# Tile 0 normalized in two parts and tile 1 in one, the bias row loaded behind W2's second half, and a new written order

## The chip, the cores and the metric

The kernel runs on one core of one Trainium2 chip. Its engines are TensorE (PE, with its weight loads shown apart as PEld), VectorE (DVE), ScalarE (ACT), GpSimd (POOL) and SyncE (SP), which issues nearly all DMAs. The metric is the device time of one execution in microseconds (us); lower is better.

## The reference

```python
def _A_ref(x, w_r, w_i):                  # x: 2048 x 640
    X = rfft2(x.astype(float32), axes=(-2, -1))
    X = X * (w_r + 1j * w_i)              # 2048 x 321
    return irfft2(X, s=(S, D), axes=(-2, -1)).astype(bfloat16)

def _B_ref(x, w1, b1, w2, b2):
    h = gelu_tanh(einsum("bsd,df->bsf", x, w1) + b1)    # 640 -> 1536
    return einsum("bsf,fd->bsd", h, w2) + b2            # 1536 -> 640

xn = layernorm(x)                         # over the 640 columns
return x + _A_ref(xn, A_w_r, A_w_i) + _B_ref(xn, B_w1, B_b1, B_w2, B_b2)
```

All inputs and outputs are bf16. The output is the input plus a spectral filter of the normalized input plus a two-layer network on the normalized input.

## The kernel before

The 2048 rows are 16 tiles of 128 rows, two tiles to a pair. Each step has a name, and the names carry tile, group or block numbers:

- `x4` loads tiles of the input; `w1_00` to `w1_14` load W1 in ten chunks (half, fifth of the contraction); `w2_0` and `w2_1` load W2 in two halves; `bias2` loads b2 to all partitions; `W..` load the spectral weights.
- `st`, `ag` (DVE) are mean and variance; `sq`, `rs` the reciprocal deviation (for tiles 0 and 1 on ACT and DVE, later on POOL); `nm` (line 555, DVE) subtracts the mean and multiplies, and writes the normalized tile.
- A normalized tile is transposed: tiles 0 to 3 on PE (`tp`, line 569) into a PSUM bank, which `tc` (line 423 on ACT or 424 on DVE) copies to xnT; tiles 4 to 15 by DMA (`td`, line 561).
- `h` are the matmuls of the first layer. Blocks 0 and 1 are single tiles, and their matmuls have 128 columns: `h0.2.1` is block 0, bank 2 of four, fifth 1 of the contraction, three matmuls. Later blocks have two or four tiles. `ge` (ACT) are the gelus, `b1mm` and `b1cp` bring the bias b1 into place for them.
- `f1`, `f2` (DVE), `G` (PE), `gx`, `b`, `xb`, `c`, `y`, `m`, `z`, `d`, `u`, `vt`, `e`, `yo`, `y2`, `yf` are the spectral path, forward and back.
- `k` (ten tiles, early) and `l` (six tiles, late) are the matmuls of the second layer, `kk` (DVE) parks a `k` result with the residual added; `fin` (PE) is the last spectral step of one piece of a tile, `os` (line 810, DVE) adds it up into one of four staging slots, and `out` (SP) stores it. A tile's `os` waits until the store that used its slot before has landed.

Every step is recorded with what it reads and writes. The order of the steps on each engine is not found by a scheduler when the program is built: it is written out by hand in the table `ORDER` (engine and name, one after the other), and a second table, `SLOTS`, gives each step its PSUM bank or buffer slot. From these the program works out the semaphore waits. An engine runs its list strictly in order, so a waiting step holds all that is behind it. A `gate` bears on what order is admissible and gives no wait of its own.

Before the first real matmul, PE runs nine matmuls on zeros (`idle0`).

Of the kernel before, what the change touches and what calls it, by code (L numbers as in the profile page):

```python
# [13 lines left out]
D = 640  # L14
# [228 lines left out]
PARTS = (0, 1, 3, 5)  # L243
# [10 lines left out]
pool:xbpad2b sp:x0 dve:warm0 act:bias1 pool:xbpad0b dve:eps5 pool:xbpad1a pool:id0 pe:idle0 pool:id1 act:table0 sp:x1 pool:xbpad1b pool:xbpad2a  # L254
pool:wpad sp:w1_00 pool:mhalf pool:xbpad0a sp:w1_01 sp:w1_02 sp:x2 dve:st0.0 dve:st0.1 sp:w1_03 dve:st1.0 sp:w1_04 dve:ag0 dve:st1.1 sp:x3 act:sq0
dve:rs0 sp:w1_10 pe:b1mm dve:ag1 dve:nm0 dve:nm0.1 act:sq1 pe:tp0.0 act:b1cp dve:nm0.3 sp:w1_11 pe:tp0.1 dve:rs1 dve:tc0.0 pe:tp0.3 dve:nm1.1
act:tc0.1 sp:w1_12 pe:h0.0.0 dve:nm1 dve:nm1.3 pe:tp1.1 act:tc0.3 pe:h0.1.0 sp:w1_13 dve:f10.1 pe:tp1.0 act:tc1.1 pe:tp1.3 pe:h0.1.1 act:tc1.0
pe:h0.0.1 dve:f10.0 sp:w1_14 act:table1 pe:h0.0.2 pe:h1.0.0 dve:st2.0 sp:x4 pe:h1.0.1 pe:h1.0.2 pe:h0.1.2 dve:st2.1 sp:x6 pe:h0.1.3 pe:h0.0.3
dve:f20.00 pe:h0.1.4 sp:g act:tc1.3 pe:h1.1.0 dve:ag2 pe:h1.1.1 dve:st3.0 sp:x8 pe:h1.1.2 pe:h1.0.3 dve:ve2 pe:h1.0.4 dve:st3.1 sp:x10 pool:rs2
pe:h1.2.0 pe:h0.3.0 act:ge1.1 pe:h0.2.0 sp:x12 dve:ag3 act:ge1.0 pe:h0.2.1 dve:f20.11 dve:ve3 pe:h1.1.3 act:ge0.3 dve:nm2 pe:h1.2.1 pool:rs3 act:ge1.2  # L260
pe:h1.3.0 dve:f20.10 pe:h1.3.1 act:ge0.4 pe:h1.3.2 dve:f20.01 pe:h1.3.3 dve:nm3 pe:tp2.0 pe:h1.1.4 dve:f11.0 pe:h0.2.2 act:tc2.0 pe:h1.2.2 pe:h1.2.3
dve:f11.1 pe:h0.0.4 act:ge1.4 pe:h0.3.1 pe:tp3.0 dve:st4.0 pe:h0.3.2 dve:st5.1 pe:h0.3.3 act:tc3.0 pe:h1.2.4 pe:h1.3.4 dve:st5.0 pe:h0.3.4 act:ge0.5
pe:h0.2.3 dve:st4.1 pe:h2.0.0 act:ge0.0 act:ge0.1 dve:ag5 pe:h2.0.3 dve:ag4 act:ge0.11 pe:h0.2.4 dve:ve4 pe:h2.4.0 dve:st6.0 act:ge1.6 pool:rs4
pe:h2.4.3 act:ge1.5 dve:st6.1 pe:h2.1.0 act:ge1.3 act:ge0.10 pe:h2.1.3 dve:nm4 act:ge0.7 pe:h2.5.0 dve:st7.1 act:ge1.8 sp:td4 pe:h2.2.0 act:ge1.11
dve:nm5 pe:h2.2.3 act:ge1.7 pe:h2.3.0 dve:f21.10 act:ge0.8 pe:h2.3.3 dve:ag6 dve:st8.0 pe:h2.6.0 act:ge2.3 sp:td5 pe:h2.6.3 dve:st7.0 pe:h2.5.3
act:ge2.2 pe:h2.7.0 dve:f21.00 act:ge0.9 pe:h2.7.3 dve:f21.01 act:ge0.6 dve:f21.11 pe:h2.10.0 dve:ag7 act:ge0.2 dve:st11.1 sp:x14 pe:h2.10.3 act:ge2.7
pe:h2.11.0 dve:st10.1 sp:w2_0 act:ge2.6 pe:h2.11.3 dve:f12.0 act:ge2.4 pe:G0 sp:W10n dve:ve6 pe:h2.8.0 act:ge2.5 dve:st8.1 pool:rs6 pe:G1 act:ge2.0
dve:st12.1 pe:h2.8.3 dve:nm6 act:ge2.1 pe:h2.9.0 dve:nm7 act:ge2.10 pe:h2.9.3 dve:st10.0 pe:h3.0.0 act:gx0.0 pe:h3.6.0 pe:h3.0.3 dve:st11.0 sp:td7
pe:h3.1.0 dve:ag10 pe:h3.6.3 dve:f12.1 act:ge2.9 pe:h3.7.0 act:ge2.8 dve:ag11 dve:f22.00 pe:h3.7.3 pe:G3 dve:ve10 sp:td6 dve:st9.1 act:ge3.7 pe:h3.4.0
pool:rs10 act:ge2.11 dve:st9.0 pe:h3.4.3 pe:h3.5.0 act:ge3.6 dve:f22.10 pe:h3.5.3 dve:f22.11 pe:G2 dve:f22.01 dve:st14.0 pe:h3.1.3 act:gx1.0 pe:h3.8.0  # L270
dve:ag9 dve:nm10 pe:h3.8.3 pe:h3.10.0 dve:nm11 sp:td10 pe:h3.10.3 dve:ag8 pe:h3.11.0 act:ge3.0 dve:ve8 dve:f13.0 pool:rs8 pe:h3.11.3 act:ge3.1
dve:f13.1 pe:G5 act:ge3.4 pe:G4 sp:td11 dve:nm8 act:ge3.5 pe:h3.2.0 dve:f23.00 pe:h3.2.3 act:gx2.0 pe:h3.3.0 dve:nm9 pe:h3.9.0 dve:st12.0 sp:td8
pe:h3.9.3 dve:f23.10 pe:k1.0.0 act:ge3.9 dve:f23.11 dve:f23.01 pe:h3.3.3 dve:st13.0 act:ge3.8 pe:k1.0.3 act:ge3.3 dve:st15.0 sp:td9 pe:k2.0.0
act:ge3.11 dve:st15.1 act:ge3.2 pe:G7 dve:st14.1 pe:G6 act:ge3.10 dve:f14.1 pe:h4.6.0 sp:bias2 act:ge1.10 dve:f14.0 pe:h4.6.3 act:ge1.9 sp:w2_1
pe:h4.7.0 act:gx3.0 dve:f24.10 pe:h4.4.0 sp:W10m dve:st13.1 pe:h4.7.3 pe:h4.4.3 dve:ag12 sp:m pe:k2.0.3 dve:f24.00 act:ge4.7 dve:f24.11 sp:W12p
act:ge4.6 dve:f24.01 pe:h4.5.0 dve:ag13 dve:ag14 pe:h4.5.3 dve:f15.0 sp:W00p pe:h4.10.0 act:ge4.5 dve:f15.1 pe:h4.10.3 pe:h4.11.0 act:ge4.4 sp:W13p
dve:ve12 dve:f25.01 pool:rs12 dve:f25.00 pe:h4.11.3 pe:G8 sp:e dve:f25.10 act:ge4.11 pe:G9 dve:f25.11 sp:W11n act:ge4.10 pe:h5.0.0 dve:nm13 act:gx4.0
# [56 lines left out]
def bass_parallel_sum__spectral_gfnet__dense_activation_gelu__prompt_kernel(  # L334
# [516 lines left out]
```

## Time and profile before

| what | value |
|---|---|
| device time, median of 3 runs | 148.06 us (147.77 to 148.54) |
| profiled execution: its own time | 147.68 us |
| profiled execution: span from first to last instruction | 146.2 us |
| PE busy | 142.7 us, 98% of the span |
| DVE busy | 117.8 us, 81% |
| ACT busy | 80.8 us, 55% |
| DMA | 18.39 MB, mean 126 GB/s |

Busy time counts an instruction from its start to its end, and matmuls overlap, so a busy PE is no proof that it ran at its peak. In the rows below a timeline row gives start, duration, engine, line, operation, output and input, shape, count and, in brackets, the idle time before it and what ended it. A row of the chain of waits gives start, duration, and what the end of the program was then waiting for. A group row gives count, busy time, mean duration of one in ns, and idle time before it.

### The profile page before, as it was taken

Reading aid. Unit: us, or ns where it says so; the run is one execution under the profiler, and the core shown is the slowest. Engines: PE = TensorE matmul, PEld = TensorE weight load, DVE = VectorE, ACT = ScalarE, POOL = GpSimd, SP = SyncE. Lnnn points to the kernel's source line nnn. Section 1 sums busy time; section 2 is a strip of 40 time slices with the busy share of each in tenths; the row PEclk is TensorE's granted clock in tenths of the full one; section 3 lists DMA queues with packets and bytes.
Section 4 is the critical chain, followed back from the end, with each engine's and each line's share of the span. In section 5 each row is a group of like instructions: output and inputs, shape, how many; then the busy total and the mean of one; then the engine's idle time right before and its main releaser. Section 6 shows DMA issues by size and latency. Waiting matters only on the chain.

```text
span 146.2 us, 4123 instructions
## 1 busy us (share of the span) xinstructions
PE 142.7 (98%) x1727; PEld 96.2 (66%) x1727; DVE 117.8 (81%) x274; ACT 80.8 (55%) x154; POOL 6.8 (5%) x24
## 2 busy tenths in 40 slices
PE   7999999999999999999999999999999999999994
PEld 2589899887567867545555443446787767767773
DVE  2999999999879625639999888973179999699994
ACT  3586998998664735473884778774044622400000
POOL 2030111201200000000000000000000000000000
PEclk9999999999999999999999999999999999999999
DMA  4999679757999999300000677546600003031145
GB/s 141 278 348 399 196 197 289 146 104 223 242 132 208 182 160 189 121 0 4 0 4 2 42 140 121 69 90 134 125 14 0 4 0 112 25 131 53 66 159 179
DMA packets 29369, 18.39 MB, mean 126 GB/s; under 512 B 20264, under 2 KB 28200, under 8 KB 29224
## 3 DMA queue, kind: packets, MB, share of 16 engines
q1 hardware_dynamic: 29328, 18.14, 53.7%
q8 instruction: 13, 0.21, 0.6%
q14 instruction: 4, 0.03, 0.1%
q10 hardware_dynamic: 24, 0.00, 0.0%
HBM read 10.92 MB, written 2.62 MB: 93 GB/s over the span
## 4 chain that ended last, share of the span: by engine, by line
PE 92%; DMA 3%; SPq 3%; issue 0%; DVE 0%
PE ps L413 91%; DMA W<-in_B_w_dram 3%; SPq L408 3%; PE ps L569 0%; DVE W L810 0%
## 5 line engine op out<-in xcount | busy, mean ns | idle before, releaser
L413 PE MATMUL ps<-W,gT 128*128 128x384 bf16 (+3 forms) x396 | 59.5, 296 | 0.0
L413 PE MATMUL ps<-xnT,W 128*128 128x256 bf16 (+2 forms) x420 | 59.0, 289 | 0.1
L413 PEld LDWEIGHTS ps<-W,gT 128*128 128x128 bf16 x396 | 36.4, 98 | 17.5 <-issue 1.9
L413 PEld LDWEIGHTS ps<-xnT,W 128*128 128x128 bf16 x420 | 34.6, 98 | 14.6 <-issue 1.2
L639 ACT ACTIVATE gT<-ps,b1col 128x256 bf16<-128x256 f32 (+2 forms) x84 | 36.9, 522 | 7.0 <-PE ps L413 6.9
L523 DVE BATCH_NORM_STATS2 U<-X 128x6 f32<-128x320 bf16 x32 | 14.0, 478 | 2.2 <-DMA X<-in_A_x_dram 2.1
L800 DVE TENSOR_TENSOR xnT<-ps,X 128x384 f32<-128x384 f32 (+1 forms) x16 | 7.8, 485 | 7.1 <-PE ps L413 7.1
L423 ACT ACTIVATE T<-ps 128x644 bf16<-128x644 f32 (+2 forms) x19 | 10.5, 595 | 5.0 <-PE ps L413 4.8
L423 ACT ACTIVATE Wf<-ps 128x960 bf16<-128x960 f32 (+1 forms) x8 | 6.7, 867 | 9.8 <-PE ps L413 9.8
L423 ACT ACTIVATE XV<-ps 128x1280 bf16<-128x1280 f32 (+1 forms) x8 | 9.6, 1202 | 0.5 <-PE ps L413 0.4
L584 DVE TENSOR_TENSOR T<-T 128x512 bf16<-128x512 bf16 (+1 forms) x32 | 9.0, 315 | 0.1
L423 ACT ACTIVATE Xb<-ps 128x960 bf16<-128x960 f32 x4 | 5.1, 1265 | 6.4 <-PE ps L413 6.4
L810 DVE TENSOR_TENSOR W<-ps,xnT 128x256 bf16<-128x256 f32 (+1 forms) x16 | 7.4, 485 | 0.7 <-PE ps L413 0.5
L555 DVE TENSOR_SCALAR T<-X,mv,rstd 128x640 bf16<-128x640 bf16 (+2 forms) x20 | 7.4, 406 | 0.7 <-POOL rstd L534 0.6
L424 DVE CAST T<-ps 128x644 bf16<-128x644 f32 x5 | 4.1, 827 | 4.7 <-PE ps L413 4.7
L413 PE MATMUL ps<-Wf,htab 128*128 128x384 bf16 (+3 forms) x33 | 7.5, 295 | 0.0
L699 DVE TENSOR_TENSOR T<-T 128x644 bf16<-128x644 bf16 x16 | 7.4, 488 | 0.2
L413 PE MATMUL ps<-EB,XV 32*128 32x160 bf16 (+1 forms) x128 | 7.2, 232 | 0.0
L580 DVE TENSOR_TENSOR T<-T 128x640 bf16<-128x640 bf16 x16 | 7.1, 479 | 0.1
L534 POOL TENSOR_TENSOR rstd<-ve,mhalf 128x2 f32<-128x2 f32 (+1 forms) x8 | 5.7, 710 | 31.0 <-DVE ve L533 31.0
L768 DVE TENSOR_TENSOR Wf<-Wf 128x960 bf16<-128x960 bf16 (+1 forms) x12 | 6.9, 596 | 0.1
L413 PEld LDWEIGHTS ps<-EB,XV 32*128 32x128 bf16 (+1 forms) x128 | 5.6, 95 | 2.1 <-ACT U L423 0.4
(62 smaller groups left out, 127.3 us busy)
## 6 DMA issues: line engine op xcount, KB each, us to landing
out_dram<-W SPq DMA_DIRECT2D x15, 160.0 KB, 1.9
W<-in_B_w_dram SPq DMA_DIRECT2D x10, 192.0 KB, 4.4
X<-in_A_x_dram SPq DMA_DIRECT2D x6, 320.0 KB, 6.0
W<-in_B_w_dram SPq DMA_DIRECT2D x2, 960.0 KB, 8.4
Wf<-in_A_w_i_dram SPq DMA_DIRECT2D x7, 160.5 KB, 5.5
Wf<-in_A_w_r_dram SPq DMA_DIRECT2D x7, 160.5 KB, 5.4
X<-in_A_x_dram SPq DMA_DIRECT2D x4, 160.0 KB, 3.3
gtab<-c_G SPq DMA_DIRECT2D x1, 512.0 KB, 6.3
```

Of the source, the lines that this page charges most:

```text
L413: ins = e.matmul(o_, lhsT=lw, rhs=rh, start=st, stop=sp_, skip_group_check=True)
L423: return e.activation(dst(), src(), ACT.Copy)
L523: K.op(f"st{c}.{h}", "dve", lambda e, _, c=c, h=h: e.bn_stats(stats[:, c, 6 * h:6 * h + 6], view(X, c * D + H2 * h, [[1, H2]])), reads=[B_ ...
L534: K.op(f"rs{c0}", "pool", lambda e, _, a=a, b=b: e.tensor_tensor(out=rstd[:, a:b], in0=ve[:, a:b], in1=mhalf[:, a:b], op=ALU.pow), reads=[ ...
L555: norm = K.op(f"nm{c}.{a // 128}" if a else f"nm{c}", "dve", lambda e, _, c=c, n=n, a=a, b=b, xnv=xnv: e.tensor_scalar(out=xnv(n, a, [[1, ...
L580: K.op(f"f1{pair}.{k}", "dve", lambda e, _, k=k, op=op, xnv=xnv, x1v=x1v: e.tensor_tensor(out=x1v(H2 * k, [[D, 2], [1, H2]]), in0=xnv(0, 0 ...
L584: ring_ops.append(K.op(f"f2{pair}.{k}{i}", "dve", lambda e, _, op=op, x1v=x1v, xfv=xfv, o_=o_, o0=o0, o1=o1, w=w: e.tensor_tensor(out=xfv( ...
L639: K.op(f"ge{bi}.{fc}", "act", lambda e, _, c0=c0, nt=nt, fc=fc, f0=f0, hps=hps: e.activation(gT[:, fc, 128 * c0:128 * (c0 + nt)], psb(hps. ...
L699: return e.tensor_tensor(out=rows, in0=rows, in1=view(TT, TB.slot * 4 * KP + r * KP, [[2 * KP, 2], [1, KP]]), op=op)
L768: K.op(f"y2{gi}.{k}", "dve", lambda e, _, k=k, op=op, yo=yo, y2=y2, n=n: e.tensor_tensor(out=view(Wf, Y2 + y2.slot * 3 * D + (H2 - 1) * k, ...
L800: K.op(f"kk{c}.{o0}", "dve", lambda e, _, kps=kps, c=c, home=home, o0=o0, w=w: e.tensor_tensor(out=home[:, o0 // 128:(o0 + w) // 128], in0 ...
L810: K.op(f"os{c}.{o0}", "dve", lambda e, _, c=c, os_=os_, fps=fps, o0=o0, w=w, kept=kept, home=home if kept else None: e.tensor_tensor(out=( ...
```

## The change

Tile 0 was normalized in three pieces (columns 0 to 127, 128 to 383, 384 to 639) and tile 1 likewise. Now tile 0 is normalized in two pieces, columns 128 to 639 first and then 0 to 127, and tile 1 in one. The transposes of tiles 0 and 1 keep their three turns each (one, two and two blocks of 128 columns). The row b2 is issued behind the second half of W2 where it was issued ahead of it. `ORDER` and `SLOTS` are written anew from the first to the last step; of them a line or two stands here.

```diff
 ORDER = """
-pool:xbpad2b sp:x0 dve:warm0 act:bias1 pool:xbpad0b dve:eps5 pool:xbpad1a pool:id0 pe:idle0 pool:id1 act:table0 sp:x1 pool:xbpad1b pool:xbpad2a
+pool:xbpad1b dve:warm0 act:bias1 sp:x0 pool:xbpad2a dve:eps5 pool:xbpad1a pool:xbpad0a pe:idle0 pool:xbpad0b pool:xbpad2b pool:wpad pool:id0
...
-        load("bias2", "sp", view(b2bc, 0, [[1, D]]), bass.AP(tensor=b2v.tensor, offset=b2v.offset, ap=[[0, 128], [1, D]]), B_b2b, gate=xlast)
+        load("bias2", "sp", view(b2bc, 0, [[1, D]]), bass.AP(tensor=b2v.tensor, offset=b2v.offset, ap=[[0, 128], [1, D]]), B_b2b, gate=B_w2[1].writers[:1])
...
-                parts = [(128 * a, 128 * b) for a, b in zip(PARTS, PARTS[1:])] if c < 2 else [(0, D)]
+                parts = [(0, 128), (128, D)] if c == 0 else [(0, D)]
+                turns = list(zip(PARTS, PARTS[1:])) if c < 2 else [(0, 5)]
...
-                for k, (j0, j1) in enumerate((a // 128, b // 128) for a, b in parts):
+                for k, (j0, j1) in enumerate(turns):
...
-                    tp = K.op(f"tp{c}.{j0}", "pe", xt, reads=[B_xn[k], B_id], writes=[tps])
+                    tp = K.op(f"tp{c}.{j0}", "pe", xt, reads=[B_xn[min(k, len(parts) - 1)], B_id], writes=[tps])
```

Three places of the new order matter below. The rows name line, operation, output and input, and shape, with the semaphores that an instruction waits for; the lines from 556 on are one higher after the change.

**PE, the start.** The rows at line 569 or 570 are the transposes of tiles 0 and 1, those at line 413 with `xnT,W` the first layer. Before:

```order
L569 MATMUL ps<-EB,T 128x128 [waits s_dve] x2
L569 MATMUL ps<-EB,T 128x128
L569 MATMUL ps<-EB,T 128x128 [waits s_dve]
L569 MATMUL ps<-EB,T 128x128
L413 MATMUL ps<-xnT,W 128x128 [waits d_w1_00,s_act,s_dve]
L413 MATMUL ps<-xnT,W 128x128 x2
L569 MATMUL ps<-EB,T 128x128 [waits s_dve]
L569 MATMUL ps<-EB,T 128x128
L413 MATMUL ps<-xnT,W 128x128 x3
L569 MATMUL ps<-EB,T 128x128 [waits s_dve] x2
L569 MATMUL ps<-EB,T 128x128
L413 MATMUL ps<-xnT,W 128x128 [waits d_w1_01,s_act]
```

and now:

```order
L570 MATMUL ps<-EB,T 128x128 [waits s_dve]
L570 MATMUL ps<-EB,T 128x128
L570 MATMUL ps<-EB,T 128x128 [waits s_dve]
L570 MATMUL ps<-EB,T 128x128 x2
L570 MATMUL ps<-EB,T 128x128 [waits s_dve,s_act]
L570 MATMUL ps<-EB,T 128x128 x4
L413 MATMUL ps<-xnT,W 128x128 [waits d_w1_00,s_act]
L413 MATMUL ps<-xnT,W 128x128 x2
L413 MATMUL ps<-xnT,W 128x128 [waits d_w1_01]
L413 MATMUL ps<-xnT,W 128x128 x8
L413 MATMUL ps<-xnT,W 128x128 [waits s_act]
L413 MATMUL ps<-xnT,W 128x128 x2
```

All ten transposes now stand ahead of the first matmul of the first layer. The first of tile 1's (the row with two semaphores) waits for the copy that empties the bank it takes over from tile 0.

**PE, around the second half of W1.** Before:

```order
L413 MATMUL ps<-xnT,W 128x128 [waits d_w1_04]
L413 MATMUL ps<-xnT,W 128x128 x11
L413 MATMUL ps<-xnT,W 128x128 [waits s_act]
L413 MATMUL ps<-xnT,W 128x128 x5
L413 MATMUL ps<-xnT,W 128x128 [waits d_w1_10]
L413 MATMUL ps<-xnT,W 128x128 x8
L413 MATMUL ps<-xnT,W 128x128 [waits d_w1_11]
L413 MATMUL ps<-xnT,W 128x128 x14
L413 MATMUL ps<-xnT,W 128x128 [waits d_w1_12]
```

and now:

```order
L413 MATMUL ps<-xnT,W 128x128 [waits d_w1_04]
L413 MATMUL ps<-xnT,W 128x128 x14
L413 MATMUL ps<-xnT,W 128x128 [waits d_w1_10]
L413 MATMUL ps<-xnT,W 128x128 x11
L413 MATMUL ps<-xnT,W 128x128 [waits d_w1_11]
L413 MATMUL ps<-xnT,W 128x128 x8
L570 MATMUL ps<-EB,T 128x128 [waits s_act,s_dve]
L570 MATMUL ps<-EB,T 128x128 x4
L413 MATMUL ps<-xnT,W 128x128 [waits d_w1_12]
```

Counted from the first matmul of the first layer, 60 of its matmuls stood ahead of the wait for chunk `w1_11`; now 69 do.

**DVE, near the end.** Rows at line 810 or 811 are the `os` steps; 773/774 and 768/769 are `yf` and `y2`. Before:

```order
L810 TENSOR_TENSOR W<-ps,X 128x384 [waits d_out7.0,s_pe]
L810 TENSOR_TENSOR W<-ps,X 128x256
L810 TENSOR_TENSOR W<-ps,xnT 128x384 [waits d_out6.0,s_pe]
L810 TENSOR_TENSOR W<-ps,xnT 128x384 [waits d_out3.0]
L810 TENSOR_TENSOR W<-ps,X 128x384 [waits d_out4.0]
```

and now:

```order
L774 TENSOR_TENSOR Wf<-Wf 128x3x320
L811 TENSOR_TENSOR W<-ps,xnT 128x384 [waits d_out2.0]
L769 TENSOR_TENSOR Wf<-Wf 128x6x160 [waits s_dve]
L811 TENSOR_TENSOR W<-ps,xnT 128x384 [waits d_out1.0,s_pe]
L811 TENSOR_TENSOR W<-ps,xnT 128x384 [waits d_out3.0,s_pe]
L811 TENSOR_TENSOR W<-ps,X 128x256 [waits d_out6.0,s_pe]
L811 TENSOR_TENSOR W<-ps,X 128x384 [waits s_pe]
L811 TENSOR_TENSOR W<-ps,xnT 128x256
```

The wait for tile 3's store (`out3.0`) has moved from the `os` of tile 11 to the `os` of tile 5, which stands earlier. The last row is `os7.384`, whose bank `fin5.384` takes next on PE.

More of the change, by code (lines that the diff above doesn't have):

```diff
@@ L258 @@
[L258 to L265, printed above, removed]
@@ L274 @@
[L274 to L277, printed above, removed]
@@ L306 @@
-pe:l6.384.3 pe:l6.384.6 pe:l6.384.9 pe:fin6.384 pe:fin3.0 pe:fin7.384 dve:os6.384 pe:l9.0.0 dve:os3.0 sp:out6.0 pe:fin7.0 pe:fin4.0 pe:l9.0.3
-sp:out3.0 dve:os7.0 pe:l9.0.6 dve:yf4.1 pe:l9.0.9 dve:os7.384 dve:yf4.0 pe:fin4.384 sp:out7.0 pe:l12.0.9 pe:l12.384.0 dve:y23.0 pe:l12.384.3 dve:y23.1
-pe:l12.384.6 pe:l12.384.9 dve:os4.384 pe:fin13.384 pe:fin12.384 dve:os4.0 pe:fin13.0 pe:fin12.0 pe:fin11.0 dve:os13.0 pe:l14.0.0 sp:out4.0
-dve:os13.384 pe:fin5.0 pe:k10.384.0 dve:os5.0 pe:l14.0.3 dve:os11.0 pe:k10.384.3 dve:os12.0 pe:k10.384.6 pe:fin11.384 pe:l15.0.0 dve:os11.384
@@ new lines @@
+pe:tp2.0 act:ge1.4 act:ge0.2 pe:h0.3.2 pe:h1.3.2 dve:tc2.0 act:ge0.1 pe:h0.2.2 act:ge1.0 pe:tp3.0 dve:f20.00 pe:h1.3.3 pe:h0.3.3 act:tc3.0 dve:f11.1
+pe:h1.2.0 pe:h1.2.1 dve:st4.0 pe:h0.2.3 act:ge1.3 pe:h0.2.4 pe:h0.3.4 dve:st5.0 pe:h2.2.0 act:ge0.6 dve:st4.1 act:ge0.0 pe:h2.8.0 act:ge0.9 pe:h2.2.3
+dve:st5.1 act:ge0.10 pe:h2.8.3 act:ge0.11 dve:ag4 pe:h1.3.4 dve:ag5 pe:h1.2.2 act:ge0.7 pe:h2.4.0 dve:ve4 dve:st6.0 act:ge1.2 pool:rs4 pe:h2.4.3
+act:ge0.8 dve:f11.0 pe:h2.5.0 act:ge1.1 act:ge1.11 pe:h2.5.3 dve:nm4 pe:h2.3.0 act:ge2.4 dve:f21.10 pe:h1.2.3 sp:td4 pe:h1.2.4 dve:nm5 pe:h2.3.3
@@ new lines @@
+pe:l12.0.3 act:yo5.0 dve:yf2.0 pe:l12.0.6 dve:yf2.1 act:yo5.1 pe:l12.0.9 dve:y24.1 pe:fin6.0 pe:e3 dve:os6.0 dve:y24.0 pe:l6.384.0 dve:yo3.1 act:yo3.0
+pe:l6.384.3 pe:l6.384.6 pe:l6.384.9 pe:fin6.384 pe:fin7.0 pe:fin7.384 dve:os6.384 pe:l15.0.0 dve:yf4.1 pe:fin3.0 pe:l15.0.3 dve:os3.0 pe:l15.0.6
+dve:yf4.0 sp:out3.0 pe:fin4.0 sp:out6.0 pe:l9.0.0 dve:os7.0 pe:l9.0.3 dve:y23.0 pe:fin5.0 dve:os4.0 pe:l9.0.6 dve:os5.0 pe:fin13.384 pe:l9.0.9
+dve:os13.384 pe:fin13.0 pe:k10.384.0 dve:os13.0 pe:k10.384.3 pe:k10.384.6 pe:fin11.0 dve:os7.384 sp:out13.0 pe:fin5.384 pe:fin4.384 dve:y23.1
```

124 lines of the change are left out of this document (66 added, 58 removed).

## The prediction

> **What bounds the kernel now.** I read the page's busy times first, then the chain of waits, then the timeline of the start and of the end.
>
> ```profile
> PE 142.7 (98%) x1727; PEld 96.2 (66%) x1727; DVE 117.8 (81%) x274; ACT 80.8 (55%) x154; POOL 6.8 (5%) x24
> ```
>
> The chain of waits (start, duration, what):
>
> ```profile
> 5.46 4.80 DMA W<-in_B_w_dram
> 10.25 0.05 issue
> 10.30 1.35 PE ps L413 x21
> ...
> 13.21 130.83 PE ps L413 x1551
> ```
>
> The chain ends on PE. From 13.21 to 144.04 us it finds 1551 matmuls in a row and no other engine, up to the last `os`. Before that it hangs on the chunk of W1 issued at 5.46, which landed 4.80 later. PE's weight loads show the same wait:
>
> ```profile
> 10.29 1.18 PEld L413 LDWEIGHTS ps<-xnT,W 128*128 128x128 bf16 x21 [0.31 <-DMA W<-in_B_w_dram]
> ```
>
> That is 0.31 us, the only wait of PE on a load once it runs. So the change can win in two places alone: at this wait, and before PE's dense run begins. The number of matmuls and their shapes are the same; in between, the new order can only keep what there is or lose it. The start in rows of the timeline, taken in narrow windows:
>
> ```profile
> 4.99 0.82 DVE L555 TENSOR_SCALAR T<-X,mv,rstd 128x128 bf16<-128x128 bf16 x3
> 5.09 0.29 ACT L528 ACTIVATE ve<-mv,eps 128x1 f32<-128x1 f32 x1 [0.34 <-DVE mv L525]
> 5.36 0.65 PE L569 MATMUL ps<-EB,T 128*128 128x128 bf16 x3 [0.23 <-DVE T L555]
> 5.61 0.65 PE L569 MATMUL ps<-EB,T 128*128 128x128 bf16 x4
> 6.04 0.38 ACT L423 ACTIVATE xnT<-ps 128x256 bf16<-128x256 bf16 x1 [0.59 <-PE ps L569]
> 6.04 1.25 ACT L423 ACTIVATE xnT<-ps 128x256 bf16<-128x256 bf16 x4 [0.59 <-PE ps L569]
> 6.06 0.52 PE L413 MATMUL ps<-xnT,W 128*128 128x128 bf16 x3
> 6.55 0.33 PE L413 MATMUL ps<-xnT,W 128*128 128x128 bf16 x3
> 6.92 0.55 PE L413 MATMUL ps<-xnT,W 128*128 128x128 bf16 x7
> 11.76 1.17 PE L413 MATMUL ps<-xnT,W 128*128 128x128 bf16 x18
> ```
>
> The reader is to see that PE runs without gaps from 6.92 us, when six matmuls of the first layer and all ten transposes are behind it, and that the same three matmuls took 0.52 us at 6.06 and 0.33 at 6.55: PE's clock opened between.
>
> **The start, step by step.** The pieces of the normalization cost by their width:
>
> ```profile
> L555 DVE TENSOR_SCALAR T<-X,mv,rstd 128x640 bf16<-128x640 bf16 x14 | 5.8, 438 | 0.7 <-POOL rstd L534 0.6
> L555 DVE TENSOR_SCALAR T<-X,mv,rstd 128x256 bf16<-128x256 bf16 x4 | 1.3, 341 | 0.0
> L555 DVE TENSOR_SCALAR T<-X,mv,rstd 128x128 bf16<-128x128 bf16 x2 | 0.6, 311 | 0.0
> ```
>
> A piece of 512 columns lies between 341 and 438 ns, in proportion at 405. It starts at 4.99 as the first piece did and ends at 5.40, and its transposes start at 5.46 (before, 0.06 behind the first piece's end, at 5.36): 0.10 later. Two transposes at the slow clock took 0.40 with their latency (the second and third of the row of three, from 5.61 to 5.36 + 0.65), so they end at 5.86 and the copy `tc0.1` runs on ACT from 5.89 to 6.28 (0.38 a copy, 0.03 behind its transposes). On DVE `rs1` waits for the square root (5.09 + 0.29 + 0.05) and starts at 5.43; the piece of 128 columns follows, 5.51 to 5.82, and tile 1 whole, 5.73 to 6.17. PE then does three transposes of tile 0 from 5.87 and waits for `tc0.1`, whose bank it needs: 6.28 + 0.05 = 6.33. Behind that wait stand all first-layer matmuls. Five transposes of tile 1, the first at the slow clock, take 0.32, and `h0.0.0` begins at 6.65. Its copy `tc0.0` is done by 6.46 and hides.
>
> At 6.92 the old order had done six matmuls. A row of 18 takes 1.17, its last 0.22, so one starts every 0.056 us: the new order has done 4.8 by 6.92 and is **0.07 late**. The two pieces saved on tile 1 and one on tile 0 gain no more than that: DVE is ahead of PE here. The copies of tile 1, now all behind each other on ACT (0.29 apart by the row of four), end at 7.60; PE needs the last one at 6.65 + 18 x 0.056 = 7.65. That is 0 to 0.05 of cover; should it go, PE waits 0.1 at most.
>
> **The wait for W1.** `w1_11` is ordered 69 matmuls behind the start instead of 60: 6.65 + 69 x 0.056 = 10.50, and it lands at 10.25 (SP's list is the same up to there). The wait of **0.31 goes**. What is late next: the chunks behind it leave SP 0.47 apart,
>
> ```profile
> 4.98 2.33 SPq L408 DMA_DIRECT2D W<-in_B_w_dram  x5
> ```
>
> so they land at about 10.7, 11.2 and 11.7; the new order wants them at 11.3, 12.1 and 12.9 (9, 9 and 15 matmuls and five transposes each for `tp2` and `tp3`). Tiles 2 and 3 come from DVE with some 0.4 us to spare. The copy `tc2.0` moves from ACT to DVE, where no row has it:
>
> ```profile
> L423 ACT ACTIVATE xnT<-ps 128x640 bf16<-128x640 bf16 x2 | 1.4, 703 | 1.2 <-PE ps L569 1.2
> L424 DVE CAST T<-ps 128x644 bf16<-128x644 f32 x5 | 4.1, 827 | 4.7 <-PE ps L413 4.7
> ```
>
> Between 0.70 and 0.83 it ends between 12.2 and 12.35; PE wants the bank at 12.4. I take it as hidden; at the upper end its cover is 0.05.
>
> **The middle.** `bias2` behind `w2_1` costs nothing: b2 is first wanted by the sums `xs`, many microseconds later. The other way goes the load of tiles 12 and 13, which now stands between `td4` and `td5` and holds the second back by the time of such an issue:
>
> ```profile
> 15.95 2.64 SPq L561 DMA_TRANSPOSE xnT<-T  x2
> 18.64 0.58 SPq L408 DMA_DIRECT2D X<-in_A_x_dram  x1
> ```
>
> and from issue to landing, by the DMA issues:
>
> ```profile
> xnT<-T SPq DMA_TRANSPOSE x12, 2.9
> ```
>
> `td5` left at about 17.3 and would leave at 17.9 and land 2.9 later, at 20.8. PE wants it with block 3: from 6.65, 120 matmuls and ten transposes of 0.056, 60 matmuls of 0.11 and 20 of 0.056 more for the spectral path make 21.6. Cover 0.8. I put the middle at 0, with 0 to +0.3 for handoffs that come a little late.
>
> **The end.** PE's last rows (matmuls with 96 columns, then the last `os`) are the same in both orders. Ahead of them the cover is thinner now. The rows of before:
>
> ```profile
> 126.20 1.48 PE L413 MATMUL ps<-W,gT 128*128 128x256 bf16 x12
> 127.52 0.60 PE L413 MATMUL ps<-Wf,htab 128*128 128x256 bf16 x3
> 128.77 1.63 PE L413 MATMUL ps<-W,gT 128*128 128x384 bf16 x9
> ```
>
> and of DVE:
>
> ```profile
> 128.81 0.56 DVE L810 TENSOR_TENSOR W<-ps,xnT 128x384 bf16<-128x384 f32 x1
> 129.29 0.65 DVE L773 TENSOR_TENSOR Wf<-Wf 128x960 bf16<-128x960 bf16 x1
> 129.85 0.42 DVE L810 TENSOR_TENSOR W<-ps,xnT 128x256 bf16<-128x256 f32 x1
> 130.19 0.65 DVE L773 TENSOR_TENSOR Wf<-Wf 128x960 bf16<-128x960 bf16 x1
> ```
>
> Starts lie 0.48 apart behind an `os` of 384 columns, 0.34 behind one of 256 and 0.56 behind a 960-wide step; a matmul takes 0.163 (384) or 0.11 (256). `fin3.0`, the second matmul of the row at 127.52, has six more matmuls of 384 columns and two of tile 7's `fin` ahead of it now (1.25): in the clock of before it stands at 128.9, `os3.0` at 129.25 to 129.80, and its store issued at 129.83. Stores land so (all 18, issue to landing):
>
> ```profile
> DMA to landing us min/median/max: 1.5/1.9/3.8
> ```
>
> With 1.9 tile 3's store lands at 131.73. DVE reaches `os5.0`, which takes the slot, at 131.81, so it waits for nothing; `os13.384` follows at 132.29, `os13.0` at 132.78 (its `fin` is the later one), `os7.384` at 133.26 to 133.68. PE reaches `fin5.384`, which needs that bank, 23 matmuls of 384 columns and ten of 256 behind `fin3.0`, at 133.7. It fits with nothing to spare: the store may take 2.1 us. I price it at 0, with 0 to 1.7 (below).
>
> **Sum.** -0.31 + 0.07 = **-0.24** against the profiled execution's own 147.68 (146.2 of span and 1.5 around it): 147.44. The median of the three runs is 0.38 above that execution, so I forecast 148.06 - 0.24 = **147.8 us**, -0.2%. A measurement of this kernel tells about 0.5% (0.74 us) from no change.
>
> **Rivals.**
>
> *The store of tile 3 comes late, and PE waits near the end (slower).* At the longest landing, 3.8, `os5.0` starts at 133.67, `os13.384` at 134.15, `os13.0` at 134.49, `os7.384` at 134.97 to 135.39, and `fin5.384` at 135.43: 1.7 late, 149.5 us. It decides from 2.1 us on. For it speaks that the 3.8 was this very store:
>
> ```profile
> L817 SPq DMA_DIRECT2D out_dram<-W x1: 342/342/342, 128.7 to 128.7; - x1
> DMA to landing us min/median/max: 3.8/3.8/3.8
> ```
>
> and that the stretch from 127 to 134 us has an instruction fetch too (queue, packets, MB):
>
> ```profile
> q8 instruction: 1, 0.02, 1.2%
> ```
>
> Before, the 3.8 cost nothing: tile 11's `os`, the second of this row, took the slot at 134.25, and the landing was at 132.5.
>
> ```profile
> 133.78 1.01 DVE L810 TENSOR_TENSOR W<-ps,xnT 128x384 bf16<-128x384 f32 x2
> ```
>
> Against it: the store is issued 1.1 us later now, and the median of all is 1.9. The Trainium skill (DMA: Bandwidth & Descriptors, Queues, rings and completion order) says that a DMA engine turns between its queues packet by packet; by that rule a fetch holds back one engine's share of a store; the trace agrees so far, with one fetch beside the longest landing. Chance 0.15.
>
> *The clock opens later (slower).* PE now idles until 5.46 and twice more before 6.33, where the old order had put in three first-layer matmuls. If that keeps the clock shut, PE loses up to half of each further microsecond:
>
> ```profile
> 0.98 4.14 PE L413 MATMUL ps<-EB 128*128 128x512 bf16 x10 [0.98 <-DVE EB L429]
> ```
>
> The slow stretch ran from 0.98 to about 6.5, and half of that again would cost 1.4 us: 149.2. The Trainium skill (TensorE: Matmul & The Clock Gate, What's actually happening) says that the clock opens after a busy window of about 3.4 us that runs free of the program; an estimate from that page's figure is 1.7 us for a missed window, 149.5. No row shows the window. Chance 0.05.
>
> *Nothing is won.* The copies or `tc2.0` are as late as the wait was, or the next chunk of W1 is: 148.0 to 148.3, inside 0.5%. Chance 0.15.
>
> *Faster than 147.3.* The rows leave at most 0.31 at the start; the rest would have to come from the scatter of the runs, whose range is 0.77 us, or from a cost that no row shows. Chance 0.12.
>
> The forecast keeps 0.53.
>
> **The numbers.** Faster by over 0.5%: the last rival and a little of the forecast's edge, 0.15. Slower by over 0.5%: late store 0.15 and late clock 0.05, 0.20. Within: 0.65. The forecast's own range is 147.2 to 148.4 (its 0.3 of start, 0.3 of middle, and the scatter). The range for 8 in 10 reaches half of the way into the late store: 147.1 to 149.1.
>
> **What would show it.** Right: no wait of PE's weight loads on W1 near 10.5, and the chain dense from about 6.7. The start: ten transposes from 5.46 to 6.65. The end: `os5.0` without a wait on a store, the largest landing near 131 us under 2.1. Wrong: a gap on PE of over 0.3 us anywhere behind 13 us, above all at a `fin` matmul behind a DVE row at line 811, or the pair 0.52 and 0.33 of the same three matmuls standing past 7 us.

## The result: slower by 1.15%

The changed kernel takes 149.75 us (median of 6 runs, 149.2 to 152.99), the kernel before, run beside it, 147.97 (147.43 to 148.68). The ratio is 1.0115, with a 95% interval of 1.008 to 1.0151; it leaves out the run of 152.99, which had a mean granted clock of 0.989 where the other five had 0.999 to 1. The changed kernel's profiled execution took 149.2 us, of which the span is 147.9; before, 147.68 and 146.2.

PE is still the bound. The chain of waits of the changed kernel (start, duration, what) shows what stood in its way:

```profile
6.67 4.36 PE ps L413 x78
...
18.08 4.86 DMA xnT<-T
22.94 0.05 issue
22.98 41.85 PE ps L413 x435
...
106.34 3.32 DMA XV<-U
109.66 0.05 issue
109.71 35.81 PE ps L413 x348
```

Before, one stretch of 1551 matmuls ran from 13.21 to the end. Now the chain is cut at two places, each time by a transposing DMA that lands late: `td5`, issued at 18.08 and landed 4.86 later, and the last transpose of the spectral path (`vt13`), 3.32. What the first one cost, in PE's timeline and in the groups of its weight loads between 20 and 24 us:

```profile
20.87 0.72 PE L413 MATMUL ps<-gtab,T 128*128 128x128 bf16 x10
22.98 0.39 PE L413 MATMUL ps<-xnT,W 128*128 128x256 bf16 x2 [1.39 <-DMA xnT<-T]
```
```profile
L413 PEld LDWEIGHTS ps<-xnT,W 128*128 128x128 bf16 x18 | 1.7, 98 | 1.7 <-DMA xnT<-T 1.6
```

and the second, in the same groups between 109 and 110 us:

```profile
L413 PEld LDWEIGHTS ps<-getab,XV 128*128 128x128 bf16 x5 | 0.4, 148 | 0.6 <-DMA XV<-U 0.6
```

The start did come earlier. PE's timeline has all ten transposes and then the first layer:

```profile
5.39 1.28 PE L570 MATMUL ps<-EB,T 128*128 128x128 bf16 x10 [0.49 <-DVE T L556]
6.51 0.89 PE L413 MATMUL ps<-xnT,W 128*128 128x128 bf16 x13
```

The 100th matmul of the first layer starts at 12.59, where it was 13.04. So the account against the profiled execution of before is: 0.45 won at the start, about 1.6 lost at `td5` and 0.5 to 0.6 at `vt13`, which makes 1.7; the spans differ by 1.7.

### The profile page after: what moved, and what is told of

It reads as the page before. It is cut to its first block, busy times and chain, and to the rows that moved or that the text cites. A ratio compares the mean times of both kernels' runs of the same rounds, so it can differ in the third digit from the quotient of the medians.

```text
span 147.9 us, 4119 instructions
## 1 busy us (share of the span) xinstructions
PE 142.1 (96%) x1727; PEld 95.8 (65%) x1727; DVE 119.2 (81%) x271; ACT 80.9 (55%) x154; POOL 7.2 (5%) x24
## 4 chain that ended last, share of the span: by engine, by line
PE 83%; DMA 7%; DVE 6%; SPq 1%; POOL 0%; issue 0%
PE ps L413 82%; DMA xnT<-T 3%; DVE U L523 3%; DMA XV<-U 2%; DMA X<-in_A_x_dram 1%; SPq L706 1%; DVE T L556 1%; PE ps L570 1%; DVE T L585 1%; POOL rstd L534 0%; DVE xnT L801 0%; DVE T L581 0%; DVE xnT L424 0%; DVE mv L525 0%; DVE rstd L529 0%
## 5 line engine op out<-in xcount | busy, mean ns | idle before, releaser
L413 PE MATMUL ps<-W,gT 128*128 128x384 bf16 (+3 forms) x396 | 60.3, 296 | 0.0
L423 ACT ACTIVATE T<-ps 128x644 bf16<-128x644 f32 (+2 forms) x18 | 9.9, 586 | 7.1 <-PE ps L413 7.1
L423 ACT ACTIVATE XV<-ps 128x1280 bf16<-128x1280 f32 (+1 forms) x7 | 8.4, 1194 | 2.8 <-PE ps L413 2.8
L585 DVE TENSOR_TENSOR T<-T 128x128 bf16<-128x128 bf16 (+1 forms) x32 | 8.9, 313 | 0.0
L423 ACT ACTIVATE Xb<-ps 128x960 bf16<-128x960 f32 x5 | 6.1, 1257 | 4.9 <-PE ps L413 4.9
L556 DVE TENSOR_SCALAR T<-X,mv,rstd 128x640 bf16<-128x640 bf16 (+2 forms) x17 | 6.9, 431 | 1.6 <-POOL rstd L534 1.6
L424 DVE CAST T<-ps 128x644 bf16<-128x644 f32 x6 | 5.0, 829 | 4.0 <-PE ps L413 4.0
L413 PE MATMUL ps<-Wf,htab 128*128 128x384 bf16 (+3 forms) x33 | 8.0, 295 | 0.0
L423 ACT ACTIVATE T<-XV 128x384 bf16<-128x384 bf16 (+1 forms) x4 | 3.2, 832 | 7.9 <-DMA XV<-U 7.9
```

The costliest lines, as they stand in the source:

```text
L413: ins = e.matmul(o_, lhsT=lw, rhs=rh, start=st, stop=sp_, skip_group_check=True)
L423: return e.activation(dst(), src(), ACT.Copy)
L556: norm = K.op(f"nm{c}.{a // 128}" if a else f"nm{c}", "dve", lambda e, _, c=c, n=n, a=a, b=b, xnv=xnv: e.tensor_scalar(out=xnv(n, a, [[1, ...
L585: ring_ops.append(K.op(f"f2{pair}.{k}{i}", "dve", lambda e, _, op=op, x1v=x1v, xfv=xfv, o_=o_, o0=o0, o1=o1, w=w: e.tensor_tensor(out=xfv( ...
```

## The experiments

Every profile also holds PE's own instruction fetches, one packet of 16 KB each on queue 8: 13 with the 1727 matmuls of this kernel, 14 with the 1790 of e2 below. In the changed kernel one of them starts at 20.83, as a narrow window of the DMA queues (20.7 to 20.9 us) shows, while `td5` is under way:

```profile
q8 instruction: 1, 0.02, 31.7%
```

A DMA from SP lands in sixteen shares, as many as the core has DMA engines, and the trace has the time of each. For `td5`, with the last landing of the load of tiles 12 and 13 (`x12`), the start of the nearest fetch and the time at which PE was through with the work ahead (all us; e1 to e6 are the kernels told below):

```
        x12 last   td5 issued   first   15th    last    fetch    PE ready
before   17.92      17.33       19.82   19.92   19.96   23.92     21.32
after    20.75      18.08       21.26   21.38   22.94   20.83     21.43
e1       24.59      17.69       20.18   20.29   20.34   21.95
e2       21.33      18.60       21.84   21.98   22.63   14.9      21.49
e3       22.97      18.07       23.49   23.54   23.54   21.08     21.51
e4       21.18      18.45       21.70   21.83   21.84   26.4      21.04
e5                  17.87       21.69   21.78   21.78   20.85     21.49
e6       22.67      17.70       20.16   20.28   20.33   15.3
```

Three theories for the 1.15%. **A**: `x12`, issued ahead of `td5` now, used up the cover (the time by which a landing is ahead of its need), and a fetch that held one share of `td5` by 1.56 us did the damage. **B**: the place of `x12` alone did. **C**: the new order is late in general, and `td5` only the first place where it shows.

### e1: td5 ahead of x12 again

```diff
-... sp:x12 dve:st6.1 pe:h2.1.3 act:ge1.10 pe:G1 sp:td5
+... dve:st6.1 pe:h2.1.3 act:ge1.10 pe:G1 sp:td5 sp:x12
```

> The changed kernel, with one edit on SP: the load of tiles 12 and 13 is issued behind the transpose td5 instead of ahead of it, as before the change. Theory A (a PE instruction fetch held back one of td5's sixteen shares; the load ahead of td5 only used up its cover) and theory B (the load ahead of td5 holds it back by itself) both say: td5 leaves SP at about 17.5 us, lands by 20.2, PE's wait of 1.39 us at the matmul that needs it is gone, the wait of 0.5 at the first matmul on the transposed spectral data near 109 stays, and the time is 149.75 - 1.4 = 148.3 us. Theory C (the new order is late in general, td5 is only the first place where it shows): another wait of 1 us or more takes its place and the time stays above 149.3.

Measured: 148.1 us, ratio to the kernel before 1.0013 (0.9981 to 1.0044). This one swap takes back the whole loss within the interval. `td5` landed at 20.34 and PE did not wait for it. C falls. But 0.7 stayed near 109, and a new wait stood at 26.6, in PE's timeline:

```profile
26.60 0.45 PE L413 MATMUL ps<-gtab,T 128*128 128x128 bf16 x5 [0.58 <-DVE T L585]
```

DVE's timeline says what was late there:

```profile
25.38 0.49 DVE L523 BATCH_NORM_STATS2 U<-X 128x6 f32<-128x320 bf16 x1 [1.60 <-DMA X<-in_A_x_dram]
```

DVE waited 1.60 for the load of tiles 14 and 15; the fetch at 21.95 had come down on it and on `x12`, whose last share landed at 24.59, 2.07 behind the fifteenth. The fetch did not go away; it hit what was under way in its place.

### e2 and e3: the fetches moved, the order kept

The warm-up on zeros is cut finer: as many columns in more matmuls, so that every fetch comes earlier in the program. In e2 it is 72 of 64 columns (126 more PE instructions), in e3 six of 512 and 24 of 64 (42 more).

```diff
-WARM = 9
+WARM = 0
+SMALL = 72
...
-            pe(name, lambda: [(psb(b.slot, [[1, 512]]), warm, view(EB, 800, [[0, 4], [1, 128]]), True, True) for _ in range(n)], reads=[B_warm], writes=[b], **kw)
+            pe(name, lambda: [(psb(b.slot, [[1, 512]]), warm, view(EB, 800, [[0, 4], [1, 128]]), True, True) for _ in range(n)] + [(psb(b.slot, [[1, 64]]), warm, view(EB, 800, [[1, 64]]), True, True) for _ in range(SMALL)], reads=[B_warm], writes=[b], **kw)
```

> The changed kernel; its nine warm-up matmuls of 512 columns on zeros become 72 of 64 columns, the same work in 126 more PE instructions (63 more matmuls with their weight loads), so that each instruction fetch of PE comes that much earlier in the program. The order on SP is the changed one: the load of tiles 12 and 13 ahead of td5. Theory A: the second fetch starts near 15 to 17 us, before td5 is under way; all shares of td5 land together near 21.4, PE waits at most 0.2 there, and the time is near 148.3 us. Theory B: td5's last share and the wait of 1.4 us stay, and the time is near 149.75 us.

> The control for the finer warm-up: the changed kernel with six warm-up matmuls of 512 columns and 24 of 64, 42 more PE instructions. By the trace of the changed kernel the second fetch is then asked for about 1 us earlier (17.7 instead of 18.7), so it starts between 19 and 21 us, still while td5 is under way. Theory A: one share of td5 stays 1 to 1.7 us behind the other fifteen, PE waits 0.5 to 1.5 us, the time is 148.8 to 149.8 us. Theory B: wait of 1.4 us, 149.75 us. If instead the finer warm-up by itself made the gain of the kernel with 72, a third of that gain would show here and the shares of td5 would land together.

Measured: e2 149.04 us, ratio 1.0051 (1.0005 to 1.0098); e3 150.89 us, 1.0222 (1.0144 to 1.03). PE's weight loads between 20 and 24.5 us, of e2 and of e3:

```profile
L414 PEld LDWEIGHTS ps<-xnT,W 128*128 128x128 bf16 x26 | 2.5, 98 | 1.5 <-DMA xnT<-T 1.2
```
```profile
L414 PEld LDWEIGHTS ps<-xnT,W 128*128 128x128 bf16 x18 | 1.7, 98 | 2.3 <-DMA xnT<-T 2.1
```

Neither theory had it whole. With the fetch 6 us earlier (e2) the ratio fell from 1.0115 to 1.0051, half of the loss (the two intervals still overlap a little), and the wait of the weight loads from 1.6 to 1.2. Fifteen shares of `td5` landed by 21.98, half a microsecond behind PE's want, and the last at 22.63. No fetch of PE was near; one of the other instruction queue was, 8 KB at 21.26, as the DMA queues between 20.5 and 23 us show:

```profile
q14 instruction: 1, 0.01, 2.3%
```

In e3 the fetch came at 21.08, and not one share but all were late: `x12` landed at 22.97 instead of 20.75, and all sixteen shares of `td5` 0.5 behind it. For 0.75 us no DMA packet was begun, as a table of windows has it (the last two numbers are the DMA share and GB/s, both counted by the packets begun):

```profile
21.25:22.00 0.75, 0.42 (x8) 0.25 (x5) 0.75 (x3) 0.75 (x3) 0.00 (x0) 1.00 0.00 0
```

The single packets in the trace say what held the engines. `td5` moves as 640 packets of 256 bytes. Twenty-one of them, begun between 20.35 and 20.84, all ended between 22.82 and 22.85. Meanwhile the fetch ran from 21.08 to 22.02, and from 22.00 on single 256-byte packets followed each other, as from one engine that makes up for what it missed. The last packet of `x12` itself had ended at 21.08, so its late shares, too, were not waiting for their data. In the changed kernel `td5`'s last packet began at 20.93, so the fetch at 20.83 found it all but done, and one share alone was late. That is outside what A had said of e3 (one share of `td5` late), and it costs more.

The table above also shows a rule: behind `x12`, `td5` landed 0.51 to 0.52 after the last share of `x12` in all four kernels that issue it so (after, e2, e3, e4). All 392 transposes of the 14 profiles say the same: none landed less than 0.28 us behind the last share of the sixteen-share DMA that SP had issued ahead of it, while plain loads overlap (in e1 the load of tiles 14 and 15 had its first share at 22.79, `x12` its last at 24.59). It is the landing that keeps this order, not the start: in the changed kernel the packets of `td5` began at 19.75, 1.0 ahead of the last share of `x12`.

### e4: x12 between td4 and td5 in the kernel before

```diff
-... pe:h0.2.0 sp:x12 dve:ag3 ...
+... pe:h0.2.0 dve:ag3 ...
...
-... sp:td4 pe:h2.2.0 ...
+... sp:td4 sp:x12 pe:h2.2.0 ...
...
-dve:st12.1 pe:h2.8.3 dve:nm6 ... dve:st11.0 sp:td7
+pe:h2.8.3 dve:nm6 ... dve:st11.0 dve:st12.1 sp:td7
```

> The kernel before, with the load of tiles 12 and 13 issued between td4 and td5 as in the change, and the first statistics step of tile 12 moved four steps down on DVE so that it does not wait for that load. PE's instructions are untouched; the second fetch came at 23.9 us in the kernel before. Theory A: td5 lands near 21.3 with all its shares together, PE wants it at 21.3, so it waits at most 0.3 us: 148.0 to 148.3 us, no change that can be measured. Theory B: td5 lands near 22.9, PE waits 1.5 us: 149.5 us.

Measured: 148.76 us, ratio 1.0027 (0.999 to 1.0065): between the two, and not told from no change. The profile has no fetch near, all shares within 0.14, and yet PE waited:

```profile
20.49 0.71 PE L413 MATMUL ps<-xnT,W 128*128 128x256 bf16 x5
21.93 0.71 PE L413 MATMUL ps<-xnT,W 128*128 128x256 bf16 x5 [0.73 <-issue]
```

(The profile books the gap as "issue". The next weight load began at 21.90, 0.06 behind the last share of `td5`, and the ScalarE step for which it also waits had been done at 21.00.) `td5` left at 18.45 and landed at 21.84; PE stood ready at 21.04, earlier than in the kernel before, because in this execution it had not waited for W1 (below). So B has a part: the place of `x12` alone costs PE 0.9 in this profile (21.04 to 21.90). A fetch that falls in held the last share back by 1.6 in the changed kernel and by 2.1 in e1.

### e5: x12 from ScalarE's queue

```diff
-            o = load(f"x{c}", "sp", view(X, c * D, [[1, n * D]]), xv[:, c:c + n, :].rearrange("p c d -> p (c d)"), B_x[c])
+            o = load(f"x{c}", "act" if c == 12 else "sp", view(X, c * D, [[1, n * D]]), xv[:, c:c + n, :].rearrange("p c d -> p (c d)"), B_x[c])
...
-... sp:x12 ...
+... act:x12 ...
```

> The changed kernel; the load of tiles 12 and 13 is issued from ScalarE instead of SP, at the same place of the written order (near 17.4 us), so that its transfer is under way just as before but it no longer stands ahead of td5 in SP's queue. Theory D (a transposing DMA does not begin before all that was issued ahead of it on its own queue has landed: in five kernels td5 landed 0.5 us behind the last share of that load): td5 leaves at about 17.5 and lands 2.5 us later, at 20.0 to 20.3, while the load still is under way; PE does not wait, the time is 148.1 to 148.5 us. Theory B' (the load simply shares the sixteen engines with td5): td5 lands at 21.3 or later, PE waits as in the changed kernel or by 0.1 to 1.4 us, and the time is above 148.8 us.

Measured: 147.88 us, ratio 0.9995 (0.9952 to 1.0038). The time is nearer to D, the landing is that of B': `td5` landed at 21.78. (The rule that D started from holds in four kernels, not five.) The load left ScalarE at 16.55, its packets moved from 17.56 to 19.50, and now it was `td4`, issued at 16.33, that came late: its first share at 20.47, against 18.55 in the changed kernel, its last at 21.19, with `td5` 0.5 behind. So a transpose can be held back by a load on the other queue too, as this one execution shows. PE waited a little:

```profile
21.83 0.83 PE L413 MATMUL ps<-xnT,W 128*128 128x256 bf16 x6 [0.18 <-DMA xnT<-T]
```

So most of the 1.4 went, though not by the queue set free: the load was issued 0.9 earlier. What is left of D is an order of landings on one queue, and that isn't the only bound.

### e6 and e10: the remaining waits

e6 joins e1 and the warm-up of e2. e10 adds three matmuls ahead of `e0` and `e1`, the first steps of the way back:

```diff
-pe:k3.384.9 pe:e0 pe:k0.384.0 dve:yo0.1 act:yo0.0 pe:k0.384.3 pe:k0.384.6 pe:k0.384.9 dve:y20.0 pe:e1 dve:kk3.384 dve:y20.1 pe:l13.0.0 act:yo1.0
+pe:k3.384.9 dve:kk3.384 pe:k0.384.0 pe:e0 dve:yo0.1 act:yo0.0 pe:k0.384.3 pe:k0.384.6 pe:k0.384.9 dve:y20.0 dve:y20.1 pe:l13.0.0 pe:e1 act:yo1.0
```

> td5 ahead of the load of tiles 12 and 13, and the 72 warm-up matmuls of 64 columns (126 more PE instructions). With td5 first, two waits were left at places where a fetch fell into late transfers: 0.74 us near 26.6 (DVE had waited for the load of tile 14, 25.4) and 0.72 near 109 (the last spectral transpose). Theory A (these two are the work of fetches at 22.0 and 105.1): with the fetches at about 15, 29 and 101 both are gone, and the time is 146.9 to 147.6 us, below the kernel before. Rival (the new order leaves no cover there, whatever the fetches do): both waits stay within 0.3 us, and the time stays at 148.1.

> td5 first and 72 warm-up matmuls, as in the kernel that stood at 147.70 us, and three more matmuls of the second layer ahead of each of the first two inverse spectral steps e0 and e1 (with the sum kk3.384 moved up on DVE, which one of them needs). There PE had waited 0.37 us at e0 for the last transpose. Expected: that wait falls to 0.05 or less, PE wants e0 0.33 us later, and the time is 0.2 to 0.4 us lower, 147.3 to 147.5 us. Rival: the copies behind e0 come as much later, e1 or e4 waits in its place, and the time stays at 147.7.

Measured: e6 147.7 us, ratio 0.9973 (0.9934 to 1.0011); e10 148.11 us, 0.9995 (0.9962 to 1.0029). In e6 the wait at 26.6 is gone, as A had it, and the one at `e0` is down from 0.7 to 0.4. That rest is a fetch again: at 100.32 one fell on the transpose `vt9`, which took 4.13 against 2.65 without, and SP issued the one after the next 2.3 behind its forerunner instead of 1.3. So moving the fetches moves the loss along the row of transposes and doesn't end it. The forecast of 146.9 to 147.6 was missed by 0.1, and the interval reaches 1. In e10 the wait at `e0` is gone, and the rival came true: `e4` waited for its copies. W2's first half landed late as well (28.10, 26.77 in the changed kernel), and PE waited 0.4 for it. PE at `e4`:

```profile
113.84 0.85 PE L414 MATMUL ps<-getab,XV 128*128 128x160 bf16 x9 [0.19 <-DVE Wf L425]
```

### e7 and e12: the normalization undone

Tiles 0 and 1 in three pieces each, all else as in e1 (e7) and e6 (e12):

```diff
-                parts = [(0, 128), (128, D)] if c == 0 else [(0, D)]
+                parts = [(0, 128), (128, 384), (384, D)] if c < 2 else [(0, D)]
...
-dve:nm0.1 act:sq1 sp:w1_11 dve:rs1 pe:tp0.1 dve:nm0 dve:nm1
+dve:nm0.1 dve:nm0.3 act:sq1 sp:w1_11 dve:rs1 pe:tp0.1 dve:nm0 dve:nm1.1 dve:nm1 dve:nm1.3
```

> td5 ahead of the load of tiles 12 and 13, and tiles 0 and 1 normalized in three pieces each again, the rest of the new order kept. By the pieces' rows the last piece of tile 1 ends 0.4 us later, at about 6.55, and the first matmul of the first layer starts at 6.7 to 6.8 instead of 6.57: 0.1 to 0.3 us later at the start, and as the second half of W1 has landed by then, as much later from there on: 148.2 to 148.4 us against 148.1. If the start is not what counts (a later wait takes it up), the time is the same 148.1 us.

> td5 first and 72 warm-up matmuls, and tiles 0 and 1 normalized in three pieces each again: the normalization alone is undone against the kernel that stood at a ratio of 0.997 (147.70 us). Three more instructions on DVE ahead of the last piece of tile 1, some 0.07 to 0.15 us each: the first matmul of the first layer starts at 6.8 to 7.0 us instead of 6.63, W1 has landed by then, and everything behind is as much later: 147.9 to 148.1 us, ratio 0.998 to 1.000. If the pieces hide behind PE, the first matmul starts within 0.05 of 6.63 and the ratio is 0.997.

Measured: e7 148.46 us, ratio 1.0037 (0.9993 to 1.0082); e12 147.86 us, 0.9989 (0.9939 to 1.0038). No interval tells this from e1 and e6. The profiles of e12 and, below it, e6 do:

```profile
6.81 0.55 PE L414 MATMUL ps<-xnT,W 128*128 128x128 bf16 x7
```
```profile
6.63 0.55 PE L414 MATMUL ps<-xnT,W 128*128 128x128 bf16 x7
```

The new normalization starts the first layer 0.18 us earlier, and the 100th matmul stands 0.18 earlier too (12.72 against 12.90). In e6 the first two transposes were still 0.081 apart, in e12 0.067; against the changed kernel (0.066) the 100th matmul of e12 is 0.3 later. So the change's first part is worth some 0.2 to 0.3 us at the start, 0.1 to 0.2%. At the end of these executions nothing of it is seen: their spans are 146.3 (e12) and 146.4 (e6).

### e8, e9 and e11: the bias row, and the fetches of the kernel before

e8 is the kernel before with b2 behind W2's second half; e11 is the kernel before with the warm-up of e2 and nothing else; e9 has both.

```diff
-... sp:bias2 ... sp:w2_1 ...
+... sp:w2_1 sp:bias2 ...
```

> The kernel before, with only the bias row b2 issued behind the second half of W2. My prediction: no gain and no loss, 148.26 us within 0.3; the second half lands some 0.6 us or more earlier (41.3 in the kernel before, at the moment at which PE wanted it), and no other wait appears. Rival: that landing was a wait in a part of the executions of the kernel before (0.84 us in one profile with 42.7), so the edit by itself gains 0.2 to 0.5 us.

> The kernel before, with the bias row b2 behind W2's second half and the 72 warm-up matmuls of 64 columns. In the kernel with the bias row alone one wait of PE of 0.52 us was left late, at 133.6, behind tile 3's store, which landed 4.2 us after its issue with a fetch at 129.0. Theory A: with the fetches earlier (near 123 and 138) that store lands within 2 us, the wait falls to 0.1 or less, and the time is 0.2 to 0.5 us below the kernel with the bias row alone, 147.4 to 147.8 us. Rival: the fetches fall on other transfers that are as thinly covered, and nothing is won: 147.9 to 148.3.

> The kernel before with nothing changed but the 72 warm-up matmuls of 64 columns. If the place of the fetches decides over the kernel before as it does over the changed one, its time moves by 0.3 us or more one way or the other (down if tile 3's store and the second half of W2 come out clear, up if a transpose or W1 is hit). If its cover is wide enough, the time is 148.3 us within 0.3.

Measured: e8 147.93 us, ratio 0.9968 (0.9929 to 1.0008); e9 149.64 us, 1.0078 (1.0042 to 1.0113); e11 150.52 us, 1.0153 (1.0117 to 1.0189). The bias row at best wins a little. W2's second half landed at 37.92 in e8; in e4 and e11, where b2 stands ahead, at 42.71 and 42.47, and PE waited for it, in e11 (weight loads between 40 and 43 us):

```profile
L414 PEld LDWEIGHTS ps<-W,gT 128*128 128x128 bf16 x4 | 0.3, 98 | 1.1 <-DMA W<-in_B_w_dram 0.9
```

e11 is the plainest of the runs: the kernel before, 126 more warm-up instructions, 1.5% slower. That the finer warm-up is not slow by itself, e6 shows, which has the same. The fetches fell on a chunk of W1 (at 9.6, 0.76 at 11.90) and on stores near the end. PE's timeline of e11, and DVE's:

```profile
11.90 0.34 PE L414 MATMUL ps<-xnT,W 128*128 128x128 bf16 x3 [0.76 <-DMA W<-in_B_w_dram]
...
143.50 0.61 PE L414 MATMUL ps<-Wf,htab 128*128 128x384 bf16 x3 [1.85 <-DVE W L811]
```
```profile
142.55 0.89 DVE L811 TENSOR_TENSOR W<-ps,xnT 128x256 bf16<-128x256 f32 x2 [2.13 <-DMA out_dram<-W]
```

Fifteen shares of tile 12's store were there at 140.13, the last at 142.46; the fetch (16 KB on queue 8) had started at 140.26. DVE waited 2.13 for the staging slot, then PE 1.85 for DVE. The gain that I had expected of e9 was a loss for the same reason: its first fetch held back `w1_11` (landed at 10.80, PE waited 0.6 to 0.8). So the kernel before, too, owes its time in part to where its fetches fall.

## Why the prediction was wrong

**The step that failed** is the one on the middle: "`td5` left at about 17.3 and would leave at 17.9 and land 2.9 later, at 20.8 ... Cover 0.8. I put the middle at 0". It left at 18.08 and took 4.86. The 2.9 was the median of twelve unlike transposes. All twelve had the DMA ahead of them still open, but it was another transpose for nine and a load for three. Five of the nine took 2.6 to 2.7; of the three, the two issued at 21.45 and 37.02 took 5.55 and 8.08. The term was two: behind `x12` fifteen shares took 3.3 (0.5 behind the last share of `x12`), and the fetch added 1.56. PE was ready at 21.43, near the 21.6 of the forecast. So the cover was 0.8 against the median, 0.05 against the queue, and -1.5 with a fetch. That a load now stood ahead of a transpose was in the text, and it was priced by its issue time alone, 0.6, without its transfer.

**The gain at W1** (-0.31) was there against the profiled execution, but that wait was an accident of it. In e4 and e8, which start as the kernel before, `w1_11` landed at 9.38 and 9.76 instead of 10.25 and PE did not wait; their 100th matmul stands at 12.76 and 12.68, not at 13.04. I took one execution's wait for a cost of every run. Nor was it "the only wait of PE on a load": in the same profile the weight loads of the second layer waited 0.4 for W2's second half:

```profile
L413 PEld LDWEIGHTS ps<-W,gT 128*128 128x128 bf16 x396 | 36.4, 98 | 17.5 <-issue 1.9 <-DMA W<-in_B_w_dram 0.4 <-DVE W L810 0.3
```

**The start** (+0.07 late) was a little too pessimistic: with that wait left out, the changed kernel's 100th matmul, at 12.59, and those of e1, e2, e3, e5, e6 and e10, which start as it does (12.65 to 12.72), stand between 0.04 behind and 0.17 ahead of those two. The normalization alone is worth 0.2 to 0.3 (e12 above); by the difference, an estimate, the new order of the transposes and matmuls gives 0.1 to 0.2 of it back. The working took two of the transposes at the slow clock. In the profiled execution the clock was open before they began (two of them 0.066 apart at 5.39, where before they were 0.082 apart at 5.61), and `h0.0.0` started at 6.51; in e6 it was not, and it started at 6.63, where I had 6.65.

**The late store** (rival, 0.15) named the right cause at the wrong place. `os5.0` waited for nothing: tile 3's store landed 1.75 after its issue, within the 2.1, with the fetch at 130.85 ahead of it. The mechanism that I had seen in one store, and held for a question of that store, decided the case on a transpose instead. e11 shows it on a store as I had priced it: a share 2.3 late, 1.85 on PE (I had 1.7).

**The clock later** did not come in the profile of the changed kernel, and the loss is not due to it. But the rival is not empty. In the profile of e7, whose ten transposes also stand ahead of the first layer and wait twice, the granted clock fell to 0.50 at 7.31 for 3.41 us, which at half the clock loses 1.7 (its clock row, forty slices of 3.7 us in tenths):

```profile
PEclk9959999999999999999999999999999999999999
```

Four runs on record have a mean granted clock of 0.987 to 0.989, this one and one each of the changed kernel, e2 and e3; of the kernel before none is below 1. What sets it off is not shown. `tc2.0` on DVE took 0.49, less than both bounds (0.70 and 0.83), and hid. The wait of 0.5 at `vt13` had no place in the prediction: with the 2.65 of a transpose without a fetch it would have landed at 108.99, 0.2 ahead of PE; the fetch at 106.26 held back one share of the second transpose ahead of it by 1.9 and all of the next (first share at 108.68), and the queue handed 0.7 of that on.

The range, up to 149.1, and the chance of 0.2 for slower rested on two places. The runs found five at which PE has under 1 us of cover behind a DMA: W1's chunks, `td5`, W2's second half, the last transposes and the stores.

## What to carry to other kernels

Where PE runs without gaps, ask of every DMA on which it waits what is open ahead of it on its queue and whether the cover outlasts an instruction fetch, here 1.5 to 2.5 us; a median landing time is no cover. A transposing DMA behind a large load lands only behind the load, so issue the transpose first. And a wait, or its absence, that a single profile shows beside a thin cover can be luck: compare two executions before it becomes a term of a sum.

## What the runs showed of the hardware

- **An instruction fetch holds back one share of a store.** In 14 profiles there are 252 stores of tiles: 28 had a fetch of PE between issue and landing, and 22 of these took over 2.6 us, up to 4.27; of the other 224 four took over 2.5 us, 3.01 at most, and their median is 1.77. Of 224 spectral transposes 71 had such a fetch inside: 53 of them took over 3.0 us and 18 under 2.7. Of those without one 14 took over 3.0, each right behind one that had been hit.
- **A transpose that is hit can be late as a whole.** In the 14 profiles there are 58 groups of ten or more 256-byte packets that took over 0.8 us each and all ended within 0.05 us of each other, as in e3. In 44 of them a fetch had begun 1.7 to 2.5 us before that end; the other 14 stand between 26 and 49 us, where transposes follow large loads. This fits sixteen engines that go through a transpose in step, so that the one held back holds all; the trace doesn't name the engines.
- **The place of a fetch depends on the number of PE instructions ahead of it.** Seventy-two small matmuls for nine large ones in the warm-up moved the changed kernel from 1.0115 to 1.0051 and the kernel before from 1 to 1.0153. Changes in the number of instructions, even before the real work begins, shift every later fetch (in e2 the first came at 9.52 instead of 12.76).
- **A transposing DMA lands only behind what its queue issued before it** (0.28 us or more behind its last share, 392 transposes), and a load on ScalarE's queue held one back as well (e5).
